# Loading the last 64 rows of two weight matrices as one transfer each, and clearing an output accumulator on ScalarE ahead of the softmax sums

## The chip, the cores and the metric

The kernel runs on one core of a Trainium2 chip. The metric is the device time of one execution in microseconds (us). Before the change the median of three runs is 1098.06 us (1097.89 to 1101.56).

## What is computed

Two kinds of layer alternate, A B A B, on a batch of 8 single tokens with 448 features. A is attention with cached keys and values: 16 query heads share 8 key/value heads, over 4096 cached positions of width 256. B is a small MLP. The reference, cut to what matters here:

```python
def _A_ref(x, k_cache, v_cache, wq, wo):            # x: 8 x 1 x 448
    q = (x @ wq).reshape(B, Sq, Hq, Dh).transpose(0, 2, 1, 3)   # Hq = 16, Dh = 256
    k = jnp.repeat(k_cache, rep, axis=1)            # cache: 8 x 8 x 4096 x 256
    v = jnp.repeat(v_cache, rep, axis=1)
    p = softmax(jnp.einsum("bhqd,bhkd->bhqk", q, k) * Dh ** -0.5)
    o = jnp.einsum("bhqk,bhkd->bhqd", p, v)
    return o.transpose(0, 2, 1, 3).reshape(B, Sq, Hq * Dh) @ wo

x = x + _A_ref(_layernorm(x), A_k_cache, A_v_cache, A_wq, A_wo)
x = x + _B_ref(_layernorm(x), B_w1, B_w2, B_w3, B_w4)
x = x + _A_ref(_layernorm(x), A_k_cache, A_v_cache, A_wq, A_wo)
x = x + _B_ref(_layernorm(x), B_w1, B_w2, B_w3, B_w4)
```

B normalizes, shifts its hidden values along the token axis (with one token each group shifts to zero, so `w1` and `w2` drop out), and adds `gelu(layernorm(x) @ w3) @ w4`, where `w3` is 448 x 1792. All inputs are bfloat16. The caches hold 8 x 8 x 4096 x 256 x 2 bytes, 134 MB each, and both attention layers read both of them.

## The kernel before

**Weights.** They are loaded once and stay on chip. `wq` (448 x 4096) and `w3` (448 x 1792) have 448 rows, three full blocks of 128 and a rest of 64. The three full blocks go through `load_split` (L167), one transfer each, 128 partitions by a whole row. The rest of 64 rows is folded: its left half of columns goes to partitions 0 to 63, its right half to partitions 64 to 127 (`wblk` later picks the half). Line 811 loads the left half from the queue of SyncE (SP), line 812 the right half from the queue of ScalarE (ACT). These loads are the first of the program after the 8 rows of `x` (L809); behind them on SP's queue stand the three blocks of `wq`, five blocks of the key cache, `wo`, the three blocks of `w3`, and `w4`.

**Caches.** Keys and values come in blocks of 1 MB into 15 places (`places_t`, 15 x 4096 elements per partition). `emit_loads` (L675, L700, L703) issues them all from SP, in a fixed order, as places come free; of each batch element eleven blocks stay in their places from the first attention layer to the second, one more and a quarter of another are parked in PSUM (`store`), and the others are read again.

**Attention.** For each task (layer, batch element, pair of key/value heads) and each block: VectorE (DVE) transposes the key block in place (L713), TensorE (PE) makes the scores in PSUM (`sc`, L728), ScalarE takes the exponential and its row sums (L737), PE transposes the probabilities (L764), ACT copies them into the sparse tile `ptz` (L771, shown as `ptw`), and PE multiplies them with the value blocks (`pv`, L783). The products add up in one half of the PSUM bank `o`. There are two such halves (`o_banks`); a half is cleared before its use, since every product is added with `start=False`. The list `in_use` says which of them are taken; when both are, the program calls `step` until one is given back.

**Around it.** Chains of small operations (finish attention, project with `wo`, MLP, next query) are written as Python generators and threaded between the blocks by `step`, which takes one piece of a generator up to its next `yield` at a time. Every piece is put into the engines' queues where it stands in the program; an engine takes its instructions in order. `half` is the generator that ends the attention of one batch element for 8 of its 16 heads: `z_cols` adds up the row sums and inverts them (two `yield`s inside), line 451 builds the matrix `R`, line 457 (ACT) copies the accumulator from PSUM to `o_sb`, line 458 (DVE) clears the accumulator, line 459 gives it back, and after the next `yield` PE turns it into columns and scales it (L463). It runs 31 times.

Of the kernel before, what the change touches and what calls it, by code (L numbers as in the profile page):

```python
# [8 lines left out]
FP32 = mybir.dt.float32  # L9
# [8 lines left out]
def kernel(  # L18
# [27 lines left out]
    nc = tc.nc  # L46
# [3 lines left out]
    Dh = A_k_cache.shape[3]  # L50
# [20 lines left out]
    chn = ctx.enter_context(tc.tile_pool(name="chn", bufs=1))  # L71
# [37 lines left out]

    ptz = consts.tile([128, 520], BF16, name="ptw")  # L110
    nc.vector.memset(ptz[:], 0.0)
    ptw = ptz[:, 0:512].rearrange("p (a n w) -> p a n w", a=4, w=8)

    misc = psum.tile([128, 512], FP32, name="misc")
# [50 lines left out]
    def load_split(t, src, cols):  # L165
        for fc in range(3):
            nc.sync.dma_start(t[:, fc * cols : (fc + 1) * cols], src[fc * 128 : fc * 128 + 128, :])  # L167
# [246 lines left out]
    def z_cols(zall, gps):  # L414

        np_ = len(gps)
        zm = chn.tile([128, 4, np_], FP32, tag=f"zm{np_}")
        zs_t = chn.tile([128, 2], FP32, tag="zs")
        zs = zs_t[:, 0:np_]
        nc.vector.tensor_add(  # L420
            zs, zall[:, 0, gps[0] : gps[-1] + 1], zall[:, 1, gps[0] : gps[-1] + 1]
        )
        nc.vector.tensor_tensor(  # L423
            zm[:],
            zs.unsqueeze(1).to_broadcast([128, 4, np_]),
            usel[:].unsqueeze(2).to_broadcast([128, 4, np_]),
            ALU.mult,
        )
        yield
        z_ps = misc[:, 480 : 480 + 4 * np_].rearrange("p (n g) -> p n g", n=4)  # L430
        nc.tensor.matmul(z_ps, ones, zm[:], start=True, stop=True)  # L431
        yield
        rz = chn.tile([128, 4, np_], FP32, tag=f"rz{np_}")
        nc.vector.reciprocal(rz[:], z_ps)
        return rz
# [9 lines left out]
    def half(o_ps, zall, g8, OT):  # L445


        rz = yield from z_cols(zall, range(2 * g8, 2 * g8 + 2))

        R = chn.tile([128, 8], FP32, tag="R")  # L450
        nc.vector.tensor_mul(
            R[:].rearrange("p (g n) -> p g n", n=4),
            rz[:].rearrange("p n g -> p g n"),
            fold[:].rearrange("p (g n) -> p g n", n=4),
        )
        o_sb = chn.tile([128, Dh], FP32, tag="o_sb")
        nc.scalar.copy(o_sb[:], o_ps)
        nc.vector.memset(o_ps, 0.0)
        in_use[:] = [t for t in in_use if t is not o_ps]
        yield  # L460
        ot_ps = ot_bank[:, 32 * g8 : 32 * g8 + 16].rearrange("p (j h) -> p j h", j=2)
        for j in range(2):
            nc.tensor.matmul(  # L463
                ot_ps[:, j], o_sb[:].rearrange("p (i j) -> p j i", j=2)[:, j], R[:], start=True, stop=True
            )
        yield
        nc.vector.tensor_copy(OT[:, :, 8 * g8 : 8 * g8 + 8], ot_ps)
        yield

    in_use = []  # L470

    def first_half(b, st):

        OT = work.tile([128, 2, Hq, 1], BF16, tag="OT", bufs=1)
        st["OT"] = OT
        yield from half(st["o", 0], st["z"], 0, OT[:, :, :, 0])
        yield from add_cols(
            y_room(1)[:, 0], lambda i: OT[:, i % 2, i // 2], wo_sb, range(NB2 // 2), 1
        )
        xs = xT[:, :, b : b + 1]  # L480
        nc.vector.tensor_add(xs, xs, y_room(1)[:, 0])

    def chain(b, st):
        OT = st["OT"]
        yield from half(st["o", 1], st["z"], 1, OT[:, :, :, 0])
        yield from add_cols(
            y_room(1)[:, 1], lambda i: OT[:, i % 2, i // 2], wo_sb, range(NB2 // 2, NB2), 1
        )
        xs = xT[:, :, b : b + 1]
        nc.vector.tensor_add(xs, xs, y_room(1)[:, 1])  # L490
        yield from mlp(b, 1)
        qT = chn.tile([128, NB2], BF16, tag="qT2", bufs=2)
        yield from project_q(b, 1, qT[:].unsqueeze(2))
        state[1, b] = {"qT": qT}

    def first_last(b, st):

        yield from half(st["o", 1], st["z"], 1, OT2[:, :, :, b])
        if b == Bn - 1:
            yield from add_cols(  # L500
                st["y"],
                lambda i: OT2[:, i % 2, i // 2, MID:],
                wo_sb,
                range(NB2 // 2, NB2),
                2,
                open=(claim(st), False),
            )
# [300 lines left out]
    x_row = spare[1][:Bn, 256 : 256 + D]  # L808
    nc.sync.dma_start(x_row, A_x.rearrange("b s d -> (b s) d"))  # L809
    for t, src, cols in ((wq_sb, A_wq, HD), (w3_sb, B_w3, F)):  # L810
        nc.sync.dma_start(t[0:64, 3 * cols :], src[384:448, 0 : cols // 2])
        nc.scalar.dma_start(t[64:128, 3 * cols :], src[384:448, cols // 2 :])
    load_split(wq_sb, A_wq, HD)
    ps0 = rows_to_cols(x_row, Bn)
    nc.vector.tensor_copy(xT[:], ps0)
# [43 lines left out]
    for idx, it in enumerate(items):  # L859
# [7 lines left out]
        n, kv, c = it  # L867
# [181 lines left out]
```

## Time and profile before

| what | value |
|---|---|
| time of the runs | 1098.06 us median, 1097.89 to 1101.56 |
| span of the profiled execution, first to last instruction | 1093.6 us |
| what lies around the span, against the median | 4.5 us |
| PE busy | 674.9 us, 62% |
| DVE busy | 599.1 us, 55% |
| ACT busy | 125.9 us, 12% |
| bytes moved by DMA | 446.80 MB |
| issue of line 811 on SP's queue (`wq`, `w3`) | 0.557 us, 0.583 us |
| issue of line 812 on ACT's queue (`wq`, `w3`) | 0.541 us, 0.614 us |
| from issue to landing, rest rows of `w3` | 4.8 us (SP), 4.9 us (ACT) |
| clearing of the accumulator, L458 on DVE | 31 times 0.272 us |
| copy of the accumulator, L457 on ACT | 31 times 0.378 us (median) |

The profile shows one execution. Engine busy times add up the instructions of one engine; they overlap between engines. The share of the DMA is a mean over 16 DMA engines, counted from the time that their packets took, so it can be a little over 1 where packets overlap. A wait is put down to what released it last.

### The profile page before, as it was taken

To read this page: it belongs to the slowest core of one execution; us is meant where nothing else is said; L and a number is where in the kernel's file an instruction comes from. 1 tells how busy PE (TensorE), PEld (TensorE's weight loads), DVE (VectorE), ACT (ScalarE), POOL (GpSimd) and SP (SyncE) were. 2 spreads that over 40 slices of the span, in tenths; PEclk is the share of its full clock that TensorE was granted. 3 is DMA by queue.
4 is the path that set the end of the run, shared out by engine and by line. 5 is a ranking of instruction groups with operands and counts; after the bars stand their busy time and mean duration, and the time that the engine had idled before them with its cause. 6 is when DMAs were issued, how large, how long until landed. Compare 5 with 4: busy or idle time off the path is not lost. (4 is left out here: it accounts for less than half of the span.)

```text
span 1093.6 us, 32866 instructions
## 1 busy us (share of the span) xinstructions
PE 674.9 (62%) x15063; PEld 451.8 (41%) x15063; DVE 599.1 (55%) x1215; ACT 125.9 (12%) x362; POOL 16.3 (1%) x27
## 2 busy tenths in 40 slices
PE   3234568456864677446774467834776477767775
PEld 2123345334642355324552245522454244545554
DVE  4256564656366555555465564665637553585462
ACT  0001101110110111101021001201111101111110
POOL 0000000000000000000000000000000000000000
PEclk9986556655575556555566555665556555665565
DMA  9999999999999999999999999999999999999994
GB/s 356 394 427 419 416 403 420 420 416 407 418 423 419 406 417 422 423 419 402 419 422 423 420 401 418 423 421 417 411 416 421 420 398 419 421 411 409 421 417 188
DMA packets 62010, 446.80 MB, mean 409 GB/s; under 512 B 6568, under 2 KB 10544, under 8 KB 12336
## 3 DMA queue, kind: packets, MB, share of 16 engines
q1 hardware_dynamic: 61680, 444.32, 98.6%
q8 instruction: 118, 1.93, 0.7%
q10 hardware_dynamic: 192, 0.38, 0.2%
q14 instruction: 20, 0.16, 0.0%
HBM read 444.67 MB, written 0.01 MB: 407 GB/s over the span
## 5 line engine op out<-in xcount | busy, mean ns | idle before, releaser
L713 DVE STREAM_TRANSPOSE places<-places 128x512 uint32<-128x512 uint32 (+1 forms) x576 | 462.0, 858 | 263.1 <-DMA places<-in_A_k_cache_dram 262.7
L728 PE MATMUL sc<-places,qbd 128*8 128x128 bf16 (+1 forms) x6720 | 281.9, 309 | 217.8 <-DVE places L713 179.7
L783 PE MATMUL o<-places,ptw 128*8 128x256 bf16 x3968 | 241.9, 387 | 144.6 <-DMA places<-in_A_v_cache_dram 122.1
L728 PEld LDWEIGHTS <-qbd 128*8 128x8 bf16 x6720 | 161.2, 101 | 312.8 <-issue 136.8
L783 PEld LDWEIGHTS <-ptw 128*8 128x8 bf16 x3968 | 114.1, 109 | 192.2 <-issue 151.0
L737 ACT ACTIVATE p_n<-sc 128x256 bf16<-128x256 f32 x128 | 95.6, 747 | 763.1 <-PE sc L728 763.1
L309 PEld LDWEIGHTS <-wq_sb 128*128 128x128 bf16 x1152 | 36.0, 104 | 28.3 <-issue 18.4
L358 PEld LDWEIGHTS <-wo_sb 128*128 128x128 bf16 x1280 | 38.4, 102 | 19.8 <-issue 19.8
L332 DVE CAST qbd<-misc 32x64 bf16<-32x64 f32 x64 | 13.8, 216 | 55.6 <-PE misc L328 55.0
L309 PE MATMUL misc<-xb,wq_sb 128*128 128x1 bf16 x1024 | 34.5, 166 | 6.2 <-ACT ptw L771 3.2
L358 PE MATMUL misc<-OT,wo_sb 128*128 128x1 bf16 x1024 | 34.5, 165 | 1.2 <-issue 1.2
L737 ACT ACTIVATION_READ_ACCUMULATOR p_n<-sc 128x1 f32 x128 | 33.9, 265 | 0.0
L771 ACT CAST ptw<-misc 128x128 bf16<-128x128 f32 x64 | 17.4, 273 | 139.1 <-PE misc L764 79.1
L463 PEld LDWEIGHTS misc<-R,o_sb 128*128 128x128 f32 x124 | 26.1, 292 | 9.4 <-issue 8.6
L247 POOL TENSOR_TENSOR t<-t,nhalf 128x2 f32<-128x2 f32 (+2 forms) x20 | 14.0, 703 | 1064.9 <-DVE t L268 1064.9
L463 PE MATMUL misc<-R,o_sb 128*128 128x8 f32 x124 | 28.8, 342 | 0.1
L431 PE MATMUL misc<-zm,one 128*128 128x8 f32 (+1 forms) x66 | 18.5, 354 | 15.0 <-DVE zm L423 14.2
L755 DVE STREAM_TRANSPOSE places<-store 128x512 uint32<-128x512 uint32 x32 | 20.1, 684 | 10.7 <-PE sc L728 10.6
L431 PEld LDWEIGHTS misc<-zm,one 128*128 128x128 f32 x66 | 16.0, 300 | 21.5 <-issue 15.8
L376 PEld LDWEIGHTS <-w_sb 128*128 128x128 bf16 x560 | 17.2, 105 | 9.4 <-issue 9.2
L376 PE MATMUL misc<-xb,w_sb 128*128 128x1 bf16 (+1 forms) x560 | 18.5, 166 | 3.6 <-DVE xb L286 2.2
L748 DVE STREAM_TRANSPOSE store<-places 128x512 uint32<-128x512 uint32 x32 | 19.9, 690 | 0.9 <-DMA places<-in_A_v_cache_dram 0.8
(103 smaller groups left out, 241.9 us busy)
## 6 DMA issues: line engine op xcount, KB each, us to landing
places<-in_A_v_cache_dram SPq DMA_DIRECT2D x215, 1024.0 KB, 9.5
places<-in_A_k_cache_dram SPq DMA_DIRECT2D x146, 1024.0 KB, 9.9
places<-in_A_k_cache_dram SPq DMA_DIRECT2D x23, 2048.0 KB, 18.7
places<-in_A_v_cache_dram SPq DMA_DIRECT2D x8, 768.0 KB, 7.2
wo_sb<-in_A_wo_dram SPq DMA_DIRECT2D x1, 3584.0 KB, 27.5
wq_sb<-in_A_wq_dram SPq DMA_DIRECT2D x3, 1024.0 KB, 8.0
w_sb<-in_B_w_dram SPq DMA_DIRECT2D x1, 1568.0 KB
w_sb<-in_B_w_dram SPq DMA_DIRECT2D x3, 448.0 KB, 26.2
```

What stands on the lines that cost most here:

```text
L309: nc.tensor.matmul(q_ps[:, j * Hq + h, :], w, xbs(nb)[:, xi, :], start=(fc == 0), stop=(fc == 3),)
L358: nc.tensor.matmul(y_ps[:, fc, :], w[:, i, at : at + 128], rhs(i), start=start, stop=stop, skip_group_check=open is not None,)
L376: nc.tensor.matmul(h_ps[:, c * nb : c * nb + nb], w, xbs(nb)[:, xi, :], start=(fc == 0), stop=(fc == 3),)
L431: nc.tensor.matmul(z_ps, ones, zm[:], start=True, stop=True)
L463: nc.tensor.matmul(ot_ps[:, j], o_sb[:].rearrange("p (i j) -> p j i", j=2)[:, j], R[:], start=True, stop=True)
L713: nc.vector.transpose(w, w)
L728: nc.tensor.matmul(sc[32 * k : 32 * k + 8, 128 * x : 128 * (x + nx)], qbd[:, ep, gp].rearrange("p a h -> p (a h)"), v, start=(n == 0), sto ...
L737: nc.scalar.activation(p_sb[:, :, :, 2 * u : 2 * u + 2].rearrange("p t i x -> p x t i"), sc[:, 256 * u : 256 * u + 256].rearrange("p (x t ...
L748: nc.vector.transpose(store[n][:].bitcast(U32), slot[:].bitcast(U32)[:, 512 * n : 512 * n + 512])
L755: nc.vector.transpose(slot[:].bitcast(U32)[:, 512 * n : 512 * n + 512], store[n][:].bitcast(U32))
L771: nc.scalar.copy(ptw[:, :, :, 6:8], pt_ps.rearrange("p t k (a h) -> p a (t k) h", a=4),)
L783: nc.tensor.matmul(o_ps[32 * q : 32 * q + 8, :], ptz[:, at : at + 8], v[:, y * Dh : (y + 1) * Dh], start=False, stop=(y >= 12), skip_group ...
```

## The change

It has two parts. In the first, the rest rows of `wq` and of `w3` are loaded by one transfer each instead of two; the destination is all 128 partitions, the source is seen as (half of the columns, row, column). Both are issued from SP; ACT issues no load. In the second, `half` begins with the copy of the accumulator and its clearing, ahead of the sums of `z_cols`; the clearing is now a ScalarE copy of a zero that is broadcast from a spare column of `ptz` (its columns 512 to 519 are never written after the first memset), and the accumulator is given back there, two `yield`s earlier.

```diff
     ptz = consts.tile([128, 520], BF16, name="ptw")
     nc.vector.memset(ptz[:], 0.0)
+    zero = ptz[:, 512:513]
...
     def half(o_ps, zall, g8, OT):
+        o_sb = chn.tile([128, Dh], FP32, tag="o_sb")
+        nc.scalar.copy(o_sb[:], o_ps)
+        nc.scalar.copy(o_ps, zero.to_broadcast([128, Dh]))
+        in_use[:] = [t for t in in_use if t is not o_ps]
         rz = yield from z_cols(zall, range(2 * g8, 2 * g8 + 2))
...
-        o_sb = chn.tile([128, Dh], FP32, tag="o_sb")
-        nc.scalar.copy(o_sb[:], o_ps)
-        nc.vector.memset(o_ps, 0.0)
-        in_use[:] = [t for t in in_use if t is not o_ps]
         yield
...
     for t, src, cols in ((wq_sb, A_wq, HD), (w3_sb, B_w3, F)):
-        nc.sync.dma_start(t[0:64, 3 * cols :], src[384:448, 0 : cols // 2])
-        nc.scalar.dma_start(t[64:128, 3 * cols :], src[384:448, cols // 2 :])
+        nc.sync.dma_start(
+            t[:, 3 * cols :], src[384:448].rearrange("r (h c) -> h r c", h=2)
+        )
```

In the built program the source of the new `wq` transfer has the counts 2 x 64 x 2048 elements (outermost first) and its destination 128 x 1 x 2048; for `w3` it is 2 x 64 x 896 and 128 x 1 x 896. Before, both sides of each of the four transfers had 64 as their outermost count.

## The prediction

> **What bounds the kernel now.** I read the page first: span, engines, then the slices with the DMA rows.
>
> ```profile
> span 1093.6 us, 32866 instructions
> PE 674.9 (62%) x15063; PEld 451.8 (41%) x15063; DVE 599.1 (55%) x1215; ACT 125.9 (12%) x362; POOL 16.3 (1%) x27
> ...
> DMA  9999999999999999999999999999999999999994
> GB/s 356 394 427 419 416 403 420 420 416 407 418 423 419 406 417 422 423 419 402 419 422 423 420 401 418 423 421 417 411 416 421 420 398 419 421 411 409 421 417 188
> DMA packets 62010, 446.80 MB, mean 409 GB/s; under 512 B 6568, under 2 KB 10544, under 8 KB 12336
> ## 3 DMA queue, kind: packets, MB, share of 16 engines
> q1 hardware_dynamic: 61680, 444.32, 98.6%
> ```
>
> No compute engine is busy for more than 62% of the span, while SP's queue (q1) fills 98.6% of 16 DMA engines. Next, the busy shares in stretches of time, for where this ends:
>
> ```profile
> core 0: us, PE busy (x) PEld busy (x) DVE busy (x) ACT busy (x) POOL busy (x), PEclk, DMA share, GB/s
> 2.00:7.00 5.00, 1.41 (x7) 0.78 (x7) 2.92 (x28) 1.28 (x1) 0.87 (x1) 1.00 1.00 257
> 7.00:12.00 5.00, 0.19 (x1) 0.10 (x1) 0.51 (x3) 0.00 (x0) 0.77 (x1) 1.00 1.01 419
> 210.00:240.00 30.00, 13.77 (x302) 7.68 (x294) 15.53 (x21) 3.06 (x9) 0.00 (x0) 0.50 1.01 421
> 1075.00:1080.00 5.00, 3.11 (x96) 2.88 (x96) 0.69 (x5) 0.00 (x0) 0.00 (x0) 0.50 0.72 290
> ```
>
> The last two columns are the DMA share and GB/s. The DMA engines are full from about 2 us until the last block comes in, and are slow only from 2 to 7 us, where the small loads run. Then the end, in the chain of waits in order of time:
>
> ```profile
> 1043.67 19.21 DMA places<-in_A_k_cache_dram
> 1062.94 17.77 DMA places<-in_A_v_cache_dram
> 1080.76 0.60 PE store L797 x16
> ...
> 1090.55 0.27 DVE places L1014
> ```
>
> The last value block lands at about 1080.7 us and a tail of 12.9 us follows. So the time is 2 us of start, some 1078 us of DMA at about 420 GB/s, the tail, and 4.5 us between span (1093.6) and median (1098.06). Only what a DMA engine does, or what lets one run dry, moves the end. 420 GB/s over 16 is 26.3 GB/s for each engine.
>
> **The accumulator on ScalarE.** The source view of L457, then the waits:
>
> ```profile
> L457 ACT COPY o_sb<-o x31: 372/378/422, 94.1 to 1055.6; 128x256 f32<-128x256 f32 x31
> ...
> ACT o_sb L457 <- PE o L783: 31.9, 12, 8.0
> ...
> DVE o L458 <- ACT o_sb L457: 11.1, 8, 2.3
> ...
> PE o L783 <- DVE o L458: 9.3, 12, 1.5
> ```
>
> Removed: 31 memsets of 0.272 us on DVE, 8.4 us. Added: 31 zero copies on ACT. No row shows one; the nearest are the copy of the same size (378 ns), the smaller L771 (273 ns) and the exponential of the same size (747 ns). I take 378 ns because shape and engine are the same: 11.7 us, bounds 8.5 and 23.2, on an engine that is busy for 126 of 1094 us. Moved: the copy stands two program steps earlier. It waits for the last product into its half (12 waits, up to 8.0 us); behind it on ACT stand the next exponentials and the copies of L771. Compared queue by queue, PE's order differs in one place (16 products of one value block ahead of 16 MLP products), DVE loses its memsets and shifts a few small operations, and SP's order of loads is the same. As PE runs in order too, an exponential of later scores cannot be ready before the product the copy waits for, so ACT blocks little that could run. PE's 9.3 us of waiting for a cleared half can vanish, or grow to 31 x (0.378 + 0.378) = 23.4 us if copy and zero were both waited for each time. All of it is covered by the loads under way: a value block takes 9.5 us (median) from issue to landing, while 1 MB at 420 GB/s takes 2.5 us, so about four blocks are queued and a delay of the consumers must pass some 7 us in one piece before an engine runs dry. I cost this part at 0. Uncovered, it would be between -9.3 - 8.4 = -17.7 and +23.4 us. Of the gain at most some 4 us could be seen: that is what the DMA share lacks to its usual 1.01, added up over stretches of 10 us (0.98 at 370, 500 and 630 us, 0.99 and 1.00 in some twenty others).
>
> **The two loads.** Removed: two issues on ACT (0.54 and 0.61 us), which nobody waits for: ACT's first exponential is at 25.2 us. On SP two issues stay; the old ones took 0.56 and 0.58 us and 1 MB issues 0.43 us (median), so the blocks behind them start as before, within 0.2 us. The bytes are the same, 128 rows of 4096 B and 128 of 1792 B. What can differ is over how many engines they are spread, and here the page has a count. Its issue list has 411 transfers, of which five have 8 rows: `x` and the four outputs. The packets under 512 B are 6568. If every transfer leaves one small completion packet on each engine it uses, 406 x 16 + 5 x 8 = 6536, and the outputs' 32 rows of 224 B make it 6568 exactly. From 0 to 12 us the same count is 104 = 8 for `x` + 6 x 16 for the six transfers that landed:
>
> ```profile
> DMA packets 689, 3.39 MB, mean 283 GB/s; under 512 B 104, under 2 KB 240, under 8 KB 368
> ```
>
> So an outermost count of 8 gives 8 shares, and 64 and 128 give 16. The new loads have 128 on the chip's side but 2 outermost in the source. No row has sides that differ; the ends are 16 shares (by the destination) and 2 (by the source). I take 2: if shares are cut along the outermost step, both sides must have as many steps, and of the rows `x` is nearest, whose 8 rows were not cut into 16 shares though 896 B could be halved. By 16 the part costs 0.
>
> With two shares, the two engines carry 64 rows of each load instead of 8: 56 x (4096 + 1792) = 329,728 B more, at 26.3 GB/s 12.5 us. The trace's own packet records (medians 159 ns for 4096 B, 75 ns for 1792 B) give 56 x 0.234 = 13.1 us, which I use. Every later block is split evenly over 16 engines and is complete only with its last share, so these two engines stay behind; the other 14 wait for places. Each packet of 8192 B takes 309 ns at the least and 309 to 311 at the median, so an engine is at its own speed and cannot catch up. Two things come off. From 2 to 7 us the old loads ran at 257 instead of 419 GB/s: (419 - 257) x 5 / 419 = 1.9 us were lost to small packets from two queues, and I count them as saved (0 if the new packets are as slow). And the 16 engines do not finish together: the completion marks of the last block span 3.1 us. If both engines are early ones, up to 3.1 us are hidden, if one is the latest, none; I take 1.0, as the later of two is likely in the last third. Sum: 13.1 - 1.9 - 1.0 = +10.2 us, ends 13.1 - 1.9 - 3.1 = 8.1 and 13.1. The profiled span would be 1103.8 us, the time 1108.3. Late first is the query projection (it waits for `wq` until 14.5 us), then each key block, but SP is not held up, as places fill without it until about 45 us.
>
> The Trainium skill bears on this row. The page "DMA: Bandwidth & Descriptors", section "Why a DMA increments its semaphore by 16 and not by 1", says that the number of engines is the largest one up to 16 that divides the slowest non-unit count of both sides, which makes it 2 here and the sum +10.2 us. The same page's "Rules for kernel authors" advises one 128-partition transfer instead of two on partition halves, which alone would make it 0. That first rule speaks against this change; no row of the trace before has a transfer with unequal sides.
>
> **Rivals.** *Even spread:* the loads use 16 engines. For it: destination of 128 partitions, like all blocks with 16 completions. Against it: the source's 2. The time is 1098.06, or 1.9 us less if the start becomes smoother: 1096.2 to 1098.5, within 0.5%. This is the case on the other side, and it decides if the count of small packets of the two loads is 32 and not 4. *Faster:* even spread, and the earlier release closes the dry stretches: -1.9 - 4 = -5.9 us, 1092.2; it passes 0.5% only if all of both is won. *A stall on ACT:* the copy waits up to 8.0 us with exponentials behind it, scores are not emptied and the loads run dry. With even spread, if each of the 12 waits cost 1 us beyond the 7 us of cover, 1110; against it, only single waits come near 8 us, and the total of all is 31.9.
>
> **Numbers.** Two shares 0.86, even spread 0.09, faster 0.03 (of it 0.02 by over 0.5%), a stall 0.02. About 0.5%, 5.5 us, is what a measurement can tell from no change. Two shares and the stall lie beyond it, since 8.1 us is the least of the former: slower 0.88, within 0.5% 0.10, faster 0.02. The time is that of two shares, 1108.3. Its own ends are 1106.2 and 1111.2; the speed of a lone 4096 B stream is unmeasured (300 ns a packet instead of 159, as some take from 2 to 5 us, on 20 packets would add 2.8 us), and the runs before lie 3.7 us apart, of which I allow 2.7 below. So the range is 1103.5 to 1114: it holds nearly all of the 0.86 and leaves out even spread.
>
> **What would show it.** Right: the first product with `wq` some 10 us later than 9.5 us; the landing of the rest rows at about 12 and 17 us instead of under 7; small packets 6568 - 64 + 4 = 6508; median time to landing longer; DMA share of later slices down by about 1%; and the tail still 12 to 13 us. Wrong: 6536 small packets (two loads of 16 in place of four), the first projection at 9.5 us, or new waits of SP on ACT that stand where the DMA share falls.

## The result and the profile after

The changed kernel takes 1115.3 us (median of 4 runs, 1110.16 to 1119.62); the kernel before, run again beside it, 1099.48 us. The ratio is 1.0137, with a 95% interval of 1.0108 to 1.0167: slower by 15 us, 12 to 18. The forecast was slower by 10.2 us, 1108.3, with a range up to 1114.0.

The page of the changed kernel, first the span, the DMA rows of the 40 slices and the packet counts:

```profile
span 1114.6 us, 32832 instructions
...
DMA  6999999999999999999999999999999999999994
GB/s 213 356 423 422 420 381 409 418 421 377 410 410 420 418 410 418 420 420 396 409 421 422 421 402 416 413 422 419 405 416 420 420 405 402 417 414 401 416 418 190
DMA packets 61950, 446.80 MB, mean 401 GB/s; under 512 B 6508, under 2 KB 10484, under 8 KB 12276
...
q1 hardware_dynamic: 61780, 444.70, 97.6%
```

The bytes are the same. The count of packets under 512 B fell from 6568 to 6508: four loads that left 16 completion packets each (small packets, one from each engine that carried a share) were replaced by two that left 2 each. In the first slice the DMA engines are no longer full, and it moves 213 instead of 356 GB/s.

Two spans must not be subtracted here. In this execution the span is 1114.6 and the time 1116.45 us; in every run of this study for which both are known they lie 1.8 to 2.0 us apart. So the execution profiled before, with a span of 1093.6, took about 1095.5 us, among the fastest of its kernel, and the 4.5 us that the prediction put around the span were mostly the difference between runs. The two spans differ by 21.0 us, the medians by 15.8, the ratio says 15.

The start, in the timeline of the changed kernel (start, duration, engine, line, and in brackets how long the engine was idle and for what):

```profile
1.18 0.64 SPq L812 DMA_DIRECT2D wq_sb<-in_A_wq_dram  x1
...
1.86 0.51 SPq L812 DMA_DIRECT2D w_sb<-in_B_w_dram  x1
...
2.42 9.65 SPq L168 DMA_DIRECT2D wq_sb<-in_A_wq_dram  x3
...
12.11 10.75 SPq L701 DMA_DIRECT2D places<-in_A_k_cache_dram  x5
...
24.82 0.19 PE L310 MATMUL store<-xb,wq_sb 128*128 128x8 bf16 x1 [19.60 <-DMA wq_sb<-in_A_wq_dram]
```

and the same place of the kernel before:

```profile
9.54 0.19 PE L309 MATMUL store<-xb,wq_sb 128*128 128x8 bf16 x1 [4.31 <-DMA wq_sb<-in_A_wq_dram]
```

The first product with `wq`, the start of the query projection, moved from 9.54 to 24.82 us, by 15.3 us. It needs the first block of `wq` and not yet the rest rows (`wblk` takes those only for the fourth product): by the semaphore updates 14 shares of that block had landed by 16.6 us, and the last two only at 24.3 and 24.8, as the two engines that carried the rest rows were still behind. That is about the whole of the loss. SP was held in the issue of the first block of `wq`: of the 9.65 us of the three issues, 8.35 belong to that one, the longest of the three in this view (shortest, median, longest, in ns):

```profile
L168 SPq DMA_DIRECT2D wq_sb<-in_A_wq_dram x3: 519/692/8350, 2.4 to 11.5; - x3
```

The busy shares of the changed kernel in stretches (the last two columns are DMA share and GB/s):

```profile
2.00:7.00 5.00, 1.41 (x7) 0.78 (x7) 2.92 (x28) 1.28 (x1) 0.87 (x1) 1.00 0.10 34
7.00:11.00 4.00, 0.00 (x0) 0.00 (x0) 0.51 (x3) 0.00 (x0) 0.77 (x1) 1.00 0.13 53
...
16.00:22.00 6.00, 0.00 (x0) 0.00 (x0) 0.00 (x0) 0.00 (x0) 0.00 (x0) 1.00 1.03 302
22.00:30.00 8.00, 0.55 (x8) 0.39 (x9) 0.00 (x0) 0.00 (x0) 0.00 (x0) 1.00 1.00 417
```

From 7 to 11 us a share of 0.13 of 16 engines is two engines, and at every whole microsecond from 4 to 11 the trace's packet records show two packets under way. From 16 to 22 us all engines are busy, and yet only 302 GB/s move. The end has not changed: the last wait of the chain is again for a value block, 12.8 us before the end of the span.

```profile
1083.96 17.83 DMA places<-in_A_v_cache_dram
```

### The profile page after: what moved, and what is told of

Read it like the earlier page. It is cut to its first block, busy times and chain, and to the rows that moved or that the text cites. A ratio compares the mean times of both kernels' runs of the same rounds, so it can differ in the third digit from the quotient of the medians.

```text
span 1114.6 us, 32832 instructions
## 1 busy us (share of the span) xinstructions
PE 674.9 (61%) x15063; PEld 452.9 (41%) x15063; DVE 591.2 (53%) x1184; ACT 139.3 (12%) x393; POOL 16.4 (1%) x27
## 2 busy tenths in 40 slices
DMA packets 61950, 446.80 MB, mean 401 GB/s; under 512 B 6508, under 2 KB 10484, under 8 KB 12276
## 3 DMA queue, kind: packets, MB, share of 16 engines
q1 hardware_dynamic: 61780, 444.70, 97.6%
## 4 chain that ended last, share of the span: by engine, by line
DMA 65%; PE 14%; DVE 13%; SPq 4%; issue 3%; ACT 1%; POOL 0%; DVEq 0%; ACTq 0%
DMA places<-in_A_k_cache_dram 47%; DMA places<-in_A_v_cache_dram 16%; DVE places L714 10%; PE sc L729 7%; PE o L784 4%; SPq L168 2%; DVE store L749 2%; DMA wq_sb<-in_A_wq_dram 1%; SPq L701 1%; PE misc L359 1%; PE misc L310 1%; PE misc L464 1%; DVE qbd L333 1%; ACT p_n L738 1%; DVE places L756 0%
## 5 line engine op out<-in xcount | busy, mean ns | idle before, releaser
L450 ACT COPY o_sb<-o 128x256 f32<-128x256 f32 x31 | 11.6, 374 | 83.4 <-PE o L784 69.6
## 6 DMA issues: line engine op xcount, KB each, us to landing
places<-in_A_v_cache_dram SPq DMA_DIRECT2D x215, 1024.0 KB, 10.1
```

## The experiments

Each is told against the kernel before, which ran beside it on the same chip. The ratios have 95% intervals.

### Each part alone

The new loads, with the accumulator as before:

```diff
-        nc.sync.dma_start(t[0:64, 3 * cols :], src[384:448, 0 : cols // 2])
-        nc.scalar.dma_start(t[64:128, 3 * cols :], src[384:448, cols // 2 :])
+        nc.sync.dma_start(
+            t[:, 3 * cols :], src[384:448].rearrange("r (h c) -> h r c", h=2)
+        )
```

> The two new loads alone, the accumulator as before. Theory (two of the 16 DMA engines carry the whole rest, and everything later waits for them): +15 us against before, 12 to 18, like the full change; 6508 packets under 512 B; the first product with wq at about 25 us instead of 9.5. Rival (the forecast's 10 us come from the loads and the missing 5 from ScalarE, whose waits for the accumulator grew from 31.9 to 69.6 us): +8 to +11 us.

Ratio 1.0138 [1.0113, 1.0163], 1115.15 against 1100.14 us: +15.2 us. 6508 small packets, and the first product at 24.70 us:

```profile
24.70 0.19 PE L309 MATMUL store<-xb,wq_sb 128*128 128x8 bf16 x1 [19.47 <-DMA wq_sb<-in_A_wq_dram]
```

Within the intervals the loads alone are the whole change.

The accumulator on ScalarE, with the loads as before:

```diff
+    zero = ptz[:, 512:513]
...
+        o_sb = chn.tile([128, Dh], FP32, tag="o_sb")
+        nc.scalar.copy(o_sb[:], o_ps)
+        nc.scalar.copy(o_ps, zero.to_broadcast([128, Dh]))
+        in_use[:] = [t for t in in_use if t is not o_ps]
         rz = yield from z_cols(zall, range(2 * g8, 2 * g8 + 2))
...
-        nc.scalar.copy(o_sb[:], o_ps)
-        nc.vector.memset(o_ps, 0.0)
-        in_use[:] = [t for t in in_use if t is not o_ps]
```

> The accumulator on ScalarE alone, the four loads as before. Theory: no change, -2 to +2 us, although the waits of ScalarE's copy double, because the DMA engines stay full; 6568 packets under 512 B. Rival (ScalarE's longer waits reach the loads): +4 to +7 us and idle DMA time beyond 20 us.

Ratio 1.0006 [0.9985, 1.0027]. In its profile the clearing and the waits of the copy (engine, line, what it waited for: total, times, longest) read:

```profile
L451 ACT CAST o<-ptw x31: 375/375/375, 84.2 to 1055.2; 128x256 f32<-128x256 bf16 x31
```

```profile
ACT o_sb L450 <- PE o L784: 67.5, 15, 8.4
...
ACT o_sb L450 <- PE misc L464: 11.6, 1, 11.6
```

The waits of the copy grew from 31.9 to 79.1 us, no wait of PE for a cleared half is listed any more (9.3 us before), and the time stands still: the interval is -1.7 to +3.0 us. What changed on the engines is hidden behind loads that are under way.

### What sets the number of engines

One transfer, 128 partitions, from SP, but with 128 as the source's outermost count as well:

```diff
-        nc.sync.dma_start(t[0:64, 3 * cols :], src[384:448, 0 : cols // 2])
-        nc.scalar.dma_start(t[64:128, 3 * cols :], src[384:448, cols // 2 :])
+        nc.sync.dma_start(
+            t[:, 3 * cols :], src[384:448].rearrange("r (h c) -> (r h) c", h=2)
+        )
```

> One transfer for each rest, 128 partitions, from SP, same bytes and same rows of 4096 and 1792 B, but the source is walked row by row, then half by half, so that both sides have 128 as their outermost count (the rest rows then stand in other partitions, and the products with them are wrong). Theory (the source's outermost count of 2 sets the shares): no change against before, -2 to +1 us; 6536 small packets; first product with wq at 8.5 to 10 us. Rival (one long transfer from one queue ahead of the blocks is what costs): +10 to +16 us.

Ratio 0.9995 [0.9974, 1.0015], and the first product at 9.60 us:

```profile
9.60 0.19 PE L309 MATMUL store<-xb,wq_sb 128*128 128x8 bf16 x1 [4.38 <-DMA wq_sb<-in_A_wq_dram]
```

The small packets are 6537; the one more than expected is a packet of 72 B on the queue q14, which the page calls one of instructions. So the joining of the transfers and the loss of the second queue together cost at most the 1.6 us that this interval leaves. This kernel leaves out what the new places of the rows would need in the products, so it is a test of the loads and not yet a replacement.

All four loads of before, issued from SP:

```diff
-        nc.scalar.dma_start(t[64:128, 3 * cols :], src[384:448, cols // 2 :])
+        nc.sync.dma_start(t[64:128, 3 * cols :], src[384:448, cols // 2 :])
```

> The four loads of before, 64 partitions each, but all four issued from SP. Theory: no change, -2 to +2 us, 6568 small packets; SP issues two transfers more, about 1.1 us, so the first block of wq lands about 1 us later at most. Rival (taking the second queue away costs): +5 us or more.

Ratio 1.0009 [0.9985, 1.0034], 6568 small packets, first product at 9.49 us.

Then the count itself. Four loads of 64 partitions from SP, whose source is walked by row modulo `a` first, for `a` of 2, 4 and 8:

```diff
+        for y in range(2):
+            nc.sync.dma_start(
+                t[64 * y : 64 * y + 64, 3 * cols :],
+                src[384:448, cols // 2 * y : cols // 2 * (y + 1)].rearrange("(r a) c -> a r c", a=2),
+            )
```

> Four loads of 64 partitions as before, all from SP, but each source is walked as (even or odd row, row, column), an outermost count of 2; the rest rows then stand in other partitions and the products with them are wrong. Theory (the source's outermost count sets the shares): two engines again, 56 rows more of each size on each of them, +13 to +17 us, 6568 - 64 + 8 = 6512 small packets. Rival (it is the single transfer over 128 partitions): no change.

> As the one with 2, with an outermost count of 4 (row modulo 4). Theory: four engines carry 32 rows of each size instead of 8, 24 more; at the 15.1 us for 56 more rows that the loads alone showed, 0.27 us each, +6.5 us (4.5 to 8.5); 6520 small packets. Rival (any odd source order drops to a slow path of two engines or one): +15 us or more.

> As the one with 2, with an outermost count of 8. Theory: eight engines carry 16 rows of each size instead of 8; +2.2 us (0 to 4); 6536 small packets.

The packet counts, one line from the page of each kernel (2, 4, 8):

```profile
DMA packets 61954, 446.80 MB, mean 403 GB/s; under 512 B 6512, under 2 KB 10488, under 8 KB 12280
```

```profile
DMA packets 61962, 446.80 MB, mean 403 GB/s; under 512 B 6520, under 2 KB 10496, under 8 KB 12288
```

```profile
DMA packets 61978, 446.80 MB, mean 406 GB/s; under 512 B 6536, under 2 KB 10512, under 8 KB 12304
```

6568 less 64 plus four times 2, 4 or 8: exactly as many completions as the source's outermost count. The packet records agree without this count: before the blocks begin, 2 packets run at a time in the changed kernel, 4 in the kernel with 4 and 8 in the one with 8 (at 4 and 5 us). The times follow. The third column is the time from the first packet of the rest rows to the end of their last, from the packet records; in the kernel before it is 3.6 us:

| outermost count of the source | rows of each size on one engine | rest rows under way | first product with `wq` | ratio to before |
|---|---|---|---|---|
| 2, one transfer for each matrix (loads alone) | 64 | 18.9 us | 24.70 us | 1.0138 [1.0113, 1.0163] |
| 2, two transfers for each matrix | 64 | 20.3 us | 26.07 us | 1.0146 [1.0116, 1.0175] |
| 4 | 32 | 13.5 us | 19.50 us | 1.0091 [1.0066, 1.0115] |
| 8 | 16 | 7.8 us | 13.86 us | 1.0050 [1.0029, 1.0071] |
| 64, all from SP | 8 | 3.6 us | 9.49 us | 1.0009 [0.9985, 1.0034] |
| 128, one transfer for each matrix | 8 | 2.9 us | 9.60 us | 0.9995 [0.9974, 1.0015] |

This much of the mechanism is shown: with 64 or 128 on the chip's side, a smaller outermost count of the source sets the number of shares (a smaller count on the chip's side was not tried). And the time moves by about as much as the first product does (with 4 the product comes 10.0 us later and the ratio makes 10.0 us of 1098.37; with 8 it is 4.3 and 5.5), and by about as much as the rest rows are longer under way than the 3.6 us of before (down the table, before rounding: 15.3, 16.7, 9.9 and 4.1 us). The sizes for 4 and 8 were expected too small (6.5 and 2.2 us), because they were priced at 0.27 us for a pair of rows, one of 4096 and one of 1792 B. By the mean packets a pair took 0.30 us in the loads alone, 0.41 with 4 and 0.48 with 8. So more rows on fewer engines does not tell all: the rows are also slower than they are alone.

### Is it the start, or the two engines?

The rest of `w3` is not needed until the first MLP. Here it is issued behind `w4`, in the new form:

```diff
+    load_rest(wq_sb, A_wq, HD)          # the new form of the load
     load_split(wq_sb, A_wq, HD)
...
     nc.sync.dma_start(w4_sb[:], B_w4.rearrange("(c p) d -> p c d", p=128))
+    load_rest(w3_sb, B_w3, F)
```

> The new loads, accumulator as before, but the rest of w3 (first needed by the MLP, after 100 us) is issued behind w4 instead of at the start. Theory (two engines are late by what they carry, wherever it stands in the queue): still slower by 11 to 16 us against before. The start alone is shorter: SP is held for about 4 us less at the first block of wq, and the first product with wq comes at 17 to 20 us instead of 24.8. Rival (the cost is that SP is held and the first projection late, so what is moved behind is hidden): only +7 to +10 us.

Ratio 1.0170 [1.0139, 1.0200], +18.7 us where 11 to 16 were expected; the first product at 22.62 us, later than the 17 to 20 expected. The rival falls: what was moved behind is not hidden. Whether the loss is larger than with both rests at the start (1.0138 [1.0113, 1.0163]) the intervals leave open. SP took 0.48 us to issue the first block and was held later instead, 5.8 us at the fourth block of keys, and all 16 engines were busy early; that did not help. The busy shares of this run show why:

```profile
8.00:18.00 10.00, 0.00 (x0) 0.00 (x0) 0.32 (x2) 0.00 (x0) 0.00 (x0) 1.00 1.02 267
...
20.00:28.00 8.00, 0.77 (x16) 0.60 (x17) 0.00 (x0) 0.00 (x0) 0.00 (x0) 1.00 1.01 420
56.00:62.00 6.00, 0.00 (x0) 0.00 (x0) 0.00 (x0) 0.00 (x0) 0.00 (x0) 1.00 0.97 303
64.00:70.00 6.00, 1.03 (x16) 0.47 (x16) 0.97 (x1) 0.00 (x0) 0.00 (x0) 1.00 1.02 426
```

The first stretch is the rest of `wq` beside blocks of `wq`, the third the rest of `w3` beside blocks of keys and values. In both, all engines are busy and move 267 and 303 GB/s; as soon as the rest is through, they move over 420.

### Why the rows are slower

The trace's packet records give the durations of single packets (mean ns, and in brackets how many):

| kernel and stretch | 4096 B (rest of `wq`) | 1792 B (rest of `w3`) | 8192 B (blocks beside) |
|---|---|---|---|
| change, 6 to 10 us, two engines alone | 159 (51) | | |
| change, 12 to 14 us, others beside | 234 (19) | | 438 (63) |
| change, 16 to 20 us, others beside | | 109 (78) | 441 (129) |
| change, 24 to 26 us, rest through | | | 314 (102) |
| rest of `w3` late, 10 to 18 us | 266 (62) | | 492 (233) |

So both streams are slower beside each other: the rest rows take 1.5 to 1.7 times their 159 ns alone (for 1792 B the nearest undisturbed value is the 75 ns of the interleaved form), the blocks 1.4 to 1.6 times their 314 ns. Two reasons were put against each other: the rest rows are read with gaps (every other half row), or an engine writes them to other partitions than in a full block, where 128 partitions over 16 engines make eight for each. First gaps in the source with the usual partitions:

```diff
-        nc.sync.dma_start(t[0:64, 3 * cols :], src[384:448, 0 : cols // 2])
-        nc.scalar.dma_start(t[64:128, 3 * cols :], src[384:448, cols // 2 :])
+        nc.sync.dma_start(t[:, 3 * cols :], src[0:128, 0 : cols // 2])
```

> One transfer for each rest as in the interleaved form, 128 partitions and 16 shares, but each partition reads the left half of another row (rows 0 to 127 of the same matrix, so the rest weights are wrong): same bytes, and a source that skips every other half row. It tells apart why the rest loads' packets were slow (4096 B at 258 to 283 ns, 1792 B at 110 to 130) where they ran beside others, though they take 159 and 75 alone and 1792 B took 75 in the interleaved form. Theory D (a packet is slow where an engine writes other partitions than the eight that it writes in every full block): 4096 B at 160 to 200 ns, 1792 B at 73 to 80, time as before, -2 to +2 us. Theory S (reading half rows with gaps is slow): 250 to 300 and 110 to 130 ns.

Then no gaps, but four partitions for each engine:

```diff
+        for y in range(2):
+            nc.sync.dma_start(
+                t[64 * y : 64 * y + 64, 3 * cols :],
+                src[384 + 32 * y : 416 + 32 * y].rearrange("r (h c) -> (r h) c", h=2),
+            )
```

> Four loads of 64 partitions from SP, 16 shares, but each reads half rows that lie one behind the other in memory, without gaps (the rest rows then stand in other partitions, and the products with them are wrong). Theory D (engines write four partitions each, not their eight): slow packets, 4096 B at 250 to 300 ns, 1792 B at 110 to 130. Theory S (gaps in the source): 160 to 200 and 73 to 80 ns. Time as before for both, -2 to +2 us.

Both kernels load rest rows that their products are not made for; they test the loads alone. Ratios 1.0012 [0.9988, 1.0036] and 1.0025 [1.0000, 1.0050]; the second is +2.7 us, a little over the 2 us expected at most. The medians of the rest packets are 159 and 74 ns with gaps and the usual partitions, 270 and 133 ns without gaps and with four partitions each. The busy shares from 2 to 7 us, first of the one with gaps, then of the one with four partitions:

```profile
2.00:7.00 5.00, 1.41 (x7) 0.78 (x7) 2.92 (x28) 1.28 (x1) 0.88 (x1) 1.00 0.87 300
```

```profile
2.00:7.00 5.00, 1.41 (x7) 0.78 (x7) 2.92 (x28) 1.28 (x1) 0.88 (x1) 1.00 0.91 241
```

The other two corners of this comparison are among the kernels above: without gaps and with the usual partitions (the interleaved form) the medians are 159 and 74 ns, with gaps and four partitions each (all four loads from SP) 265 and 131 ns. The reading with gaps is not the cause. The partitions fit, with a reserve: the mean with gaps and the usual partitions is 221 and 93 ns, since some packets are still slow, and the fast kernels also differ from the slow ones in the number of transfers (two and four).

## Why the prediction was wrong

Its mechanism was right, its size was not: +10.2 us were forecast, +15.1 measured (the ratio's 1.37% of 1099.48). The time, 1115.3 us, lies 1.3 us beyond the range. That excess alone says little: the median of the kernel before was itself 1.4 us higher beside the change (1099.48) than the 1098.06 that the forecast was added to. The 4.9 us between +10.2 and +15.1 need an account: even the low end of the interval, +12, is above the forecast. Point by point:

- **What bounds the kernel**: right. The loads alone carry the change, and the growth of ScalarE's waits from 31.9 to 79.1 us moved nothing that the interval shows.
- **The accumulator at 0**: right, 1.0006 [0.9985, 1.0027]; the clearing took 375 ns for the 378 taken.
- **Two shares**: right, 6508 small packets as forecast. The rule of the Trainium skill that was named (page "DMA: Bandwidth & Descriptors", section "Why a DMA increments its semaphore by 16 and not by 1") agrees with the counts for 2, 4 and 8. The advice of the same page's "Rules for kernel authors", one 128-partition transfer instead of two halves, did no harm here where the source's outermost count allowed 16 shares (0.9995 with 128), and cost 1.4% where it was 2 (1.0138).
- **The step that failed**: "an engine is at its own speed and cannot catch up", with 13.1 us for 56 more rows of 159 and 75 ns. Those are times of packets that nothing disturbs. Between the first packet of the rest at 2.61 us and the end of its last at 21.55 us (loads alone), the two engines needed 18.9 us for 64 rows of each size, where 64 x 0.234 makes 15.0. The term is 3.9 us too small: from 11 us on, when the blocks came to all engines, the rows took 1.4 times as long or more, and one of the first packets took 0.9 us. The trace of before held a warning. Its 159 ns are the median of all 384 packets of 4096 B, of which 256 run after 1074 us, and the same median over all packets of 1792 B is 79 ns, not 75. The 128 rest rows of each size, which ran beside other loads, took 246 and 124 ns at the median. Slow packets at the start were allowed for only in the range, with 2.8 us. (Two small readings beside it change nothing: the fastest packets of 8192 B took 307 ns, not 309, and the DMA share at 370 us is 0.99, not 0.98.)
- **The lead of 1.0 us** that was taken off: not there. 13.1 + 3.9 - 1.9 = 15.1 us already is what was measured, and the shift of the first product, 15.2 to 15.3 us, arrives whole at the end. The 1.9 us saved at the start fit this sum but were not measured alone: in the interleaved form, where the rest rows are through in 2.9 us, the interval shows no gain and leaves room for 2.9 us at most. Simpler, and without that term: the rest rows were under way for 18.9 us instead of 3.6, which is 15.3 us.
- **"SP is not held up"**: wrong, by 8.35 us at the first block of `wq`. That it cost something by itself is not shown: the two engines worked on undisturbed meanwhile (159 ns), and where the first block was issued without the hold (rest of `w3` late) their rows took 266 ns and the kernel was no faster. No run takes the hold away altogether.
- **What would show it**: the rest rows landed at 16.0 and 22.5 us for the forecast 12 and 17, by the completion marks (the semaphore updates, one for each share). The median landing did not get longer for all: 10.1 us for values (9.5 before), but 8.2 for keys (9.9 before). And the DMA share did not fall by 1% in the later slices (the share of SP's queue over the whole span did, from 98.6% to 97.6%): the other 14 engines gave up their lead early, as these stretches of the changed kernel show:

```profile
0.00:10.00 10.00, 1.41 (x7) 0.78 (x7) 4.09 (x35) 1.28 (x1) 2.35 (x7) 1.00 0.09 34
10.00:20.00 10.00, 0.00 (x0) 0.00 (x0) 0.00 (x0) 0.00 (x0) 0.00 (x0) 1.00 0.89 254
...
50.00:60.00 10.00, 0.00 (x0) 0.00 (x0) 0.00 (x0) 0.00 (x0) 0.00 (x0) 1.00 0.87 299
60.00:70.00 10.00, 3.24 (x64) 1.67 (x63) 2.74 (x4) 0.77 (x2) 0.00 (x0) 1.00 1.01 426
```

In the completion marks the two engines trail the others by some 8 us at the first block of `wq` and have them beside again by 160 us.

What stays open is whether the slow packets come from the partitions alone (two shares that keep the usual partitions were not tried), and why a pair of rows is slower still on four and eight engines. No version faster than the kernel before was found; the four loads from SP are as fast, and so are the loads in the interleaved order, with products that would have to follow it.

## What to carry to other kernels

Where the DMA engines are full, count over how many of them each transfer is spread: compare the packets under 512 B with 16 times the transfers, and look at the outermost count of both sides, not at the partitions. In this case a small transfer on two engines delayed everything that is spread over sixteen by what it added to its engines, at the start of the queue and behind the weights alike. Price such a stream by packets of its own kind that ran beside other loads, and not by a median over all packets of that size; in this case that made 0.30 us for a pair of rows instead of 0.23, and up to 0.48 where more engines carried them.

## What the runs showed of the hardware that was not expected

Full engines do not mean full speed: with every DMA engine busy (share 1.02), 267 GB/s moved in place of 420 while two engines wrote 64 partitions each, and packets of 8192 B took 492 ns instead of 314. SP stood 8.35 us in the issue of one block while only two of 16 engines had work.
